# Top-k attention and a mixture of experts in one program: the routing of the first three batches is moved to earlier steps

## The chip, the cores and the metric

The kernel runs on one core of a Trainium2 chip. The metric is the device time of one execution in microseconds. Before the change it is 1211.64 us, the median of three runs (1211.17 to 1212.91). The engines are TensorE (PE), VectorE (DVE), ScalarE (ACT), GpSimd (POOL) and SyncE (SP, which issues most of the transfers); each works off its own queue in the order of the program and waits for others by semaphores.

## The reference

Two stages follow each other. The first is attention in which each query keeps its 32 highest scores; the second sends each of the 4608 rows to one of eight experts (the largest logit decides) and scales the expert's output by that expert's probability.

```python
# q, k, v: (8, 8, 576, 64); x: 4608 rows of 512
scores = scale * np.matmul(q, k.transpose(0, 1, 3, 2))
kth = np.partition(scores, -top_k, axis=-1)[..., -top_k:-top_k + 1]      # top_k = 32
scores = np.where(scores >= kth, scores, -1e9)
attn = np.exp(scores - scores.max(-1, keepdims=True)); attn /= attn.sum(-1, keepdims=True) + 1e-9
x = np.matmul(attn, v).transpose(0, 2, 1, 3).reshape(4608, 512)

logits = x @ w_gate + modality_bias[modality_id]
e_idx = np.argmax(logits, axis=1)
gate_w = softmax(logits)[np.arange(N), e_idx]
for e in range(8):                                                       # w1: 512 x 1024, w2: 1024 x 512
    out[e_idx == e] = gate_w[e_idx == e, None] * (np.maximum(x[e_idx == e] @ w1[e], 0) @ w2[e])
```

## The kernel before

Attention is cut into 288 tiles of 128 queries: a batch has four pairs of heads, a pair nine tiles, so a batch is 36 tiles. One loop over steps `i` is a software pipeline written out by hand. In step `i` PE makes the scores of tile `i + 2` and transposes the probabilities of tile `i - 9` (`TL` is 9); ACT copies the scores to SBUF, counts signs (tile `i - 3`, buffer `K`) and makes exponentials; POOL multiplies scores and signs (`pool_y`, tile `i - 4`); DVE searches the top 32 (`subs`, `chain`, `find`) and masks (`keep`, tile `i - 7`). For two of three tiles below 48 (`early`) DVE writes only a mask (`hide`), POOL adds it one step later (`hidden`, line 470) and ACT makes the masked exponentials (`masked`). Products with V (`av`) run once for four tiles of a pair (`role(u)` 3 and 7) and once for the ninth (8); those of role 7 go through a queue, `avs`, from which the next step takes them, the others run at once. Their results are copied to `xT` in the step after (`xev`).

The routing of a batch stands in the same loop, at a position `r` counted from `i - (TL + 2)` modulo 36. At `r` = 0 come the reciprocal sums and the product with the gate (`logits`), at 1 its transposes (`logit_rows`), at 2, 3, 3, 4, 4 the transposes of the five chunks of rows (`xrow`, `RXQ`). What DVE has to do with their PSUM tiles is put into `late` and runs one step after. At `r` = 2 the list of `route` goes into the queue `side`: seven DVE operations up to the one-hot rows `oh`, a `PAUSE` (the rest waits for the next step), the exponentials and `ranks` (ten small products of PE and a copy by ACT), a `PAUSE`, and nine operations up to `dest`. At `r` = 5 the scatters (`send`, an indirect transfer that POOL issues, one for each chunk) go into `posted`, or for batch 0 into `sends`; POOL issues two of them at the end of each step. Three pauses later `base` is raised and `done` sets `seen`, the number of rows that the experts may use; for batch 0 `done` follows the list of `route` at once.

The experts work in slots of 256 rows. `more_moe` starts a slot when `seen` allows it (`PB`: 2, 4 and 6 slots after one, two and three batches): `sched` chooses an expert and its rows on DVE, SP gathers the rows into `xg`, `tokens` reads them on DVE, and `expert` makes a list of PE units (transposes `xt`, 16 of `hid`, 16 of `outp`). A planner deals these units to the steps: `spare_pe` gains 3.4 (`STEP`) in a step less the estimated `cost` of the step's attention work and is held to at most 2.6 (`CAP`); units are taken while it is above zero. A unit of `hid` or `outp` counts 0.88, a step's attention work 1.00 to 4.95 (4.95 where products of role 7 and 8 meet, every ninth step). As long as nothing is seen, every step runs `keep_warm(NW)`, six products whose results nobody reads; one more such call stands ahead of the loop (line 998). After the loop the rest of the list is worked off, and the remaining six slots are done one by one with operands split into two parts (`slot`, lines 1057 and 1073).

The pool of PSUM tiles named X has three buffers in a ring; `prep` (transposes of k and q for the next pair, positions `PJ`), `av`, `logits`, `logit_rows`, `xrow` and `ranks` all take from it. DVE's work of a step is put in order by `arrange`, which knows an estimated use and delay of each kind.

Of the kernel before, what the change touches and what calls it, by code (L numbers as in the profile page):

```python
# [13 lines left out]
AF = mybir.ActivationFunctionType  # L14
# [15 lines left out]
NW = 3  # L30
# [14 lines left out]
TL = LR + 2  # L45
# [11 lines left out]
QO = 0  # L57
PJ0 = (1, 2, 3)
FAST = 7
RXQ = (2, 3, 3, 4, 4)  # L60
SNQ, RNQ = 12, 12
RLF = (0, 1)
# [13 lines left out]
def kernel(  # L76
# [13 lines left out]
    V, A, G, PE, SP = nc.vector, nc.scalar, nc.gpsimd, nc.tensor, nc.sync  # L90
    B, H, S, D = q.shape
    E, Dm, F = w1.shape
    N = B * S
    HP = H // 2
# [25 lines left out]
    PAUSE = lambda: None  # L120
# [96 lines left out]
    ohb = [const.tile([128, 5, E], BF, name=f"ohb{i}") for i in range(2)]  # L217
    for t in ohb:
        V.memset(t, 0.0)
    lgb = [const.tile([128, 5, E], FT, name=f"lgb{i}") for i in range(2)]  # L220
    for t in lgb:
        V.memset(t, 0.0)
    x5 = const.tile([128, 5, XW], FT, name="x5")
# [44 lines left out]
    bias_all = const.tile([128, B, 5, E], FT, name="bias_all")  # L268
# [85 lines left out]
    role = lambda i: (i - 1) % 9  # L354
# [31 lines left out]
    def sevac(i):  # L386
        T[i]["S"] = sb = wk.tile([128, S], FT, name="Ssb", bufs=LR + 1 + QL - QO)
        A.activation(sb.rearrange("p (a b) -> p a b", a=2), T[i]["ps"], AF.Copy, scale=0.125)  # L388
# [142 lines left out]
    def apart(s, before, reads=()):  # L531

        for o in [*before, *reads]:
            tc.declare_no_dep(s.ins, o, reason="other rows")
        before.append(s.ins)
        G.memset(spare, 0.0)
# [47 lines left out]
            late.append(lambda lt=lt, r=r, c0=c0, n=n: V.tensor_reduce(  # L584
                lg[:r, c0:c0 + n, :], lt[:r].rearrange("p c e a h -> p c e (a h)"), axis=AX.X, op=OP.add))

    def route(lg, bias, oh, x5b, wait=0):

        t5 = lambda nm: const.tile([128, 5], FT, name=nm)
        t40 = lambda nm: const.tile([128, 5, E], FT, name=nm)  # L590
        bc = lambda t: t[:, :, None].to_broadcast([128, 5, E])
        be = lambda t: t[:, None, :].to_broadcast([128, 5, E])
        l2, z, key, ez, pr, pb = t40("r_l2"), t40("r_z"), t40("r_key"), t40("r_ez"), t40("r_pr"), t40("r_pb")
        mx, km, sm, ps5 = t5("r_mx"), t5("r_km"), t5("r_sm"), t5("r_ps5")
        dest = const.tile([128, 5], I32, name="dest")
        st = {}

        def ranks():
            ps = psX.tile([128, 6, E], FT, name="X")
            st["ps"] = const.tile([128, 6, E], FT, name="r_rk")  # L600
            PE.matmul(ps[:, 0:5, :], tri, oh, start=True, stop=False, skip_group_check=True)
            for c in range(1, 5):
                PE.matmul(ps[:, c:5, :], onesb, oh[:, 0:5 - c, :], start=False, stop=False, skip_group_check=True)
            for c in range(5):
                PE.matmul(ps[:, 5, :], onesb, oh[:, c, :], start=(c == 0), stop=(c == 4), skip_group_check=True)
            A.activation(st["ps"], ps, AF.Copy)

        def send(c):
            n_ = 128 if c < 4 else 64
            apart(G.indirect_dma_start(  # L610
                out=xs[:ZROW, :], out_offset=bass.IndirectOffsetOnAxis(ap=dest[:n_, c:c + 1], axis=0),
                in_=x5b[:n_, c, :], in_offset=None), scat, reads)
            fresh.append(scat[-1])

        return [
            lambda: V.tensor_tensor(l2, lg, bias, op=OP.add),
            lambda: V.tensor_reduce(mx, l2, axis=AX.X, op=OP.max),
            lambda: V.tensor_tensor(z, l2, bc(mx), op=OP.subtract),
            lambda: V.scalar_tensor_tensor(key, z, 0.0, be(rev), op0=OP.is_equal, op1=OP.mult),
            lambda: V.tensor_reduce(km, key, axis=AX.X, op=OP.max),  # L620
            lambda: V.tensor_tensor(oh[:, 0:4, :], key[:, 0:4, :], bc(km)[:, 0:4, :], op=OP.is_equal),
            lambda: V.tensor_tensor(oh[:64, 4, :], key[:64, 4, :], km[:64, 4:5].to_broadcast([64, E]),
                                    op=OP.is_equal),
            PAUSE,
            *[PAUSE] * wait,
            lambda: A.activation(ez, z, AF.Exp),
            ranks,
            PAUSE,
            lambda: V.tensor_reduce(sm, ez, axis=AX.X, op=OP.add),
            lambda: V.tensor_scalar(sm, sm, EPS, None, op0=OP.add),  # L630
            lambda: V.reciprocal(x5b[:, :, GW], sm),
            lambda: V.tensor_tensor(pb, st["ps"][:, 0:5, :], be(base), op=OP.add),
            lambda: V.tensor_tensor(pr, pb, oh, op=OP.mult),
            lambda: V.tensor_reduce(ps5, pr, axis=AX.X, op=OP.add),
            lambda: V.tensor_scalar(dest, ps5, float(ZROW), None, op0=OP.add),
            lambda: G.tensor_scalar(x5b[:, :, TOK], tokb, 1.0, 1.0, op0=OP.mult, op1=OP.mult),
            lambda: G.tensor_scalar(tokb, tokb, float(S), 1.0, op0=OP.add, op1=OP.mult),
        ], [f for c in range(5) for f in [lambda c=c: send(c), PAUSE] + [PAUSE] * SP_[c]] + [
            lambda: V.tensor_tensor(base, base, st["ps"][:, 5, :], op=OP.add)]
# [316 lines left out]
    def keep_warm(n):  # L956

        ps = psE.tile([128, 512], FT, name="E")
        for _ in range(2 * n):
            PE.matmul(ps[:, :256].rearrange("p (a b) -> p a b", a=2), onesb, onesb[:, None, :].to_broadcast([128, 2, 128]), start=True, stop=True)  # L960
# [30 lines left out]
    for x in range(QL):  # L991
# [3 lines left out]
            qk(0, 0, qbd[0])  # L995
            keep_warm(KP)
        sevac(x)
    keep_warm(NW)
    ok = lambda x: 0 <= x < NT
    early = lambda u: u < EARLY and u % 3 != 2  # L1000
    dn_of = lambda u: den[(u // 36) % 2][:, (u // 9) % HP, role(u):role(u) + 1]
    PREP, PREP0 = dict(zip(PJ, "tkq")), dict(zip(PJ0, "tkq"))
# [107 lines left out]
    store = []  # L1110
    for i in range(LAST):
# [5 lines left out]
        p, j = divmod(i, 9)  # L1117
        u = i - TL
# [14 lines left out]
        u = i - (KL + 1)  # L1133
# [6 lines left out]
        u = i - LE  # L1140
# [6 lines left out]
        u = i - TL  # L1147
        if ok(u):
            evac(u)
        u = i - LR - 1  # L1150
# [8 lines left out]
                f()  # L1159
        cost += COST["rest"] * (len(lp) > 0)  # L1160
        part = (PREP if p else PREP0).get(j)
        if p + 1 < NPAIR and part:
            prep(p + 1, part)
            cost += COST["t" if part == "t" else "prep"]
        if p + 2 < NPAIR and j in LJ:
            load(p + 2, "kq"[LJ.index(j)])
        if j == VJ and p < NPAIR:
            load(p, "v")
        b1, r = divmod(i - (TL + 2), 36)
        b1 -= 1  # L1170
        if 0 <= b1 < B:
            if r == 0:
                chore.extend(recip(b1, den[b1 % 2]))
            early_route = lambda b: b < FAST or b == B - 1
            rl, rx = (RL, RX) if FAST <= b1 < B - 1 else (RLF, RXQ if b1 < FAST else RXF)
            if r == rl[0]:
                rows_of[b1] = logits(b1, xTs(b1))
                cost += COST["logits"]
            if r == rl[1]:
                logit_rows(b1, rows_of[b1], lgb[b1 % 2])  # L1180
                cost += COST["xrow"]
            for c in range(5):
                if rx[c] == r:
                    xrow(b1, c, xTs(b1), x5)
                    cost += COST["xrow"]
            if r == rl[1] + (1 if early_route(b1) else 2):
                steps, store = route(lgb[b1 % 2], bias_all[:, b1], ohb[b1 % 2], x5, int(FAST <= b1 < B - 1))
                side.extend(steps)

                def done(n=b1 + 1):  # L1190
                    seen[0] = n * S
                    fresh.clear()
                if b1 == 0:
                    side.extend([store.pop(), done])
            if r == max(rl[1], rx[4]) + (1 if early_route(b1) else 2):
                if b1 == 0:
                    sends.extend(f for f in store if f is not PAUSE)
                else:
                    side.extend([f if f is PAUSE else (lambda f=f: posted.append(f)) for f in
                                 ([x for x in store[:-1] if x is not PAUSE] if b1 < FAST else store[:-1])] +  # L1200
                                [PAUSE] * 3 * (b1 < FAST) + [store[-1], done])
        u = i - (TL + 1)
# [3 lines left out]
            cost += c  # L1206
        if ok(u) and role(u) in (3, 7, 8):
            f = av(u // 9, role(u), xTs(u // 36)[(u // 9) % HP])
            if role(u) == 7:
                avs.extend(f)  # L1210
            else:
                f[0][1]()
                avs.extend(f[1:])
                cost += f[0][0]
# [42 lines left out]
        small_ = []  # L1257
        quick = 0 <= b1 < FAST and r < 16
        for x in range((RNQ if quick else RN) if rush else 0):
# [15 lines left out]
        if ok(i - LR):  # L1275
            u = i - LR
# [105 lines left out]
    def slow():  # L1382
# [6 lines left out]
        with tc.For_i(0, B, 1) as b:  # L1389
# [30 lines left out]
            for part in route(lgb[0], sb[:, 0], ohb[0], x5):  # L1420
                for f in part:
                    f()
# [42 lines left out]
```

## Time and profile before

| | us |
|---|---|
| median of three runs | 1211.64 |
| the profiled execution | 1209.28 |
| its span, first to last instruction | 1207.6 |
| PE busy (products) | 1157.0 |
| DVE busy | 1104.1 |
| ACT busy | 983.4 |
| POOL busy | 677.7 |

The mean granted clock of PE over the span is 0.992. The ends of products are modelled, so a busy PE is not necessarily a PE at its peak. In the chain of work that ended last PE has 59% of the span and DVE 31%. Expert products of the loop are lines 796 and 808, those of the last six slots lines 1057 and 1073. A wait in the rows below is the idle time of an engine just before an instruction, in brackets behind it, with the one that ended it. Step numbers are not in the trace; one search of line 437 on DVE, one product of line 433 on POOL stand for one step.

### The profile page before, as it was taken

Reading aid. Unit: us, or ns where it says so; the run is one execution under the profiler, and the core shown is the slowest. Engines: PE = TensorE matmul, PEld = TensorE weight load, DVE = VectorE, ACT = ScalarE, POOL = GpSimd, SP = SyncE. Lnnn points to the kernel's source line nnn. Section 1 sums busy time; section 2 is a strip of 40 time slices with the busy share of each in tenths; the row PEclk is TensorE's granted clock in tenths of the full one; section 3 lists DMA queues with packets and bytes.
Section 4 is the critical chain, followed back from the end, with each engine's and each line's share of the span. In section 5 each row is a group of like instructions: output and inputs, shape, how many; then the busy total and the mean of one; then the engine's idle time right before and its main releaser. Section 6 shows DMA issues by size and latency. Waiting matters only on the chain.

```text
span 1207.6 us, 28111 instructions
## 1 busy us (share of the span) xinstructions
PE 1157.0 (96%) x7920; PEld 906.5 (75%) x7920; DVE 1104.1 (91%) x5562; ACT 983.4 (81%) x2015; POOL 677.7 (56%) x1256
## 2 busy tenths in 40 slices
PE   8889979999999998999999999999999999999998
PEld 6666767778677876878687777868787777589987
DVE  7999999999999999999999999999998999486772
ACT  5999978998888986998899899989998888355652
POOL 6888875564755565565656576556655666121011
PEclk9999999999999998999999999999999999999999
DMA  5653358663586637664675657665675653277750
GB/s 125 174 163 88 88 127 236 191 167 88 153 241 152 164 104 220 175 174 123 174 215 149 168 148 196 168 160 147 183 192 145 177 156 126 83 269 237 261 198 22
DMA packets 204324, 197.10 MB, mean 163 GB/s; under 512 B 104413, under 2 KB 151533, under 8 KB 204160
## 3 DMA queue, kind: packets, MB, share of 16 engines
q1 hardware_dynamic: 196880, 175.92, 54.0%
q0 software_dynamic: 6080, 19.00, 4.3%
q8 instruction: 66, 1.08, 0.4%
q14 instruction: 98, 0.80, 0.2%
q10 hardware_dynamic: 1200, 0.30, 0.1%
HBM read 118.63 MB, written 24.23 MB: 118 GB/s over the span
## 4 chain that ended last, share of the span: by engine, by line
PE 59%; DVE 31%; ACT 5%; issue 2%; DMA 1%; POOL 0%; SPq 0%; POOLq 0%; ACTq 0%; DVEq 0%
PE E L796 11%; PE E L808 11%; PE X L519 8%; DVE cand L395 8%; PE S L383 7%; PE T L491 6%; DVE mg L437 5%; DVE P L457 5%; PE X L1073 5%; PE X L1057 4%; DVE cand L406 2%; DVE cand L407 2%; PE E L1057 1%; DVE mg L408 1%; PE X L317 1%
## 5 line engine op out<-in xcount | busy, mean ns | idle before, releaser
L395 DVE MAX8 cand<-Ssb 128x8 f32<-128x96 f32 x1728 | 388.1, 244 | 1.8 <-ACT Ssb L388 1.8
L433 POOL TENSOR_TENSOR y<-Ssb,K 128x576 f32<-128x576 f32 x288 | 368.7, 1280 | 30.5 <-ACT K L427 30.1
L383 PE MATMUL S<-ks,qs 128*128 128x288 f32 x992 | 221.1, 345 | 18.7 <-ACT Ssb L388 12.9
L427 ACT ACTIVATE K<-Ssb,n 128x576 bf16<-128x576 f32 x288 | 229.9, 798 | 7.3 <-POOL y L433 6.9
L388 ACT ACTIVATE Ssb<-S 128x576 f32<-128x576 f32 x284 | 187.8, 661 | 53.5 <-PE S L383 23.8
L437 DVE MAX8 mg<-y 128x8 f32<-128x576 f32 x288 | 213.3, 741 | 4.2 <-POOL y L433 4.2
L796 PE MATMUL E<-xgT,w1b 128*128 128x256 f32 x832 | 201.1, 384 | 2.6 <-ACT hT L800 1.5
L451 ACT ACTIVATE ex<-Ssb,sm 128x576 f32<-128x576 f32 x256 | 202.3, 790 | 0.0
L383 PEld LDWEIGHTS S<-ks,qs 128*128 128x128 f32 x992 | 152.1, 190 | 66.8 <-issue 26.2
L457 DVE SCALAR_TENSOR_TENSOR P<-Ssb,kth,ex 128x576 f32<-128x576 f32 x230 | 193.7, 842 | 6.8 <-ACT ex L451 5.6
L499 ACT ACTIVATE PT<-T 128x640 f32<-128x640 f32 (+1 forms) x288 | 193.5, 672 | 5.8 <-PE T L491 5.8
L808 PE MATMUL E<-w2b,hT 128*128 128x512 f32 x416 | 194.2, 595 | 0.5 <-ACT hT L800 0.2
L491 PE MATMUL T<-idf,P 128*128 128x128 f32 x1152 | 169.5, 274 | 7.2 <-ACT P L476 6.6
L796 PEld LDWEIGHTS E<-xgT,w1b 128*128 128x128 f32 x832 | 151.0, 190 | 29.5 <-ACT hT L800 7.4
L480 POOL TENSOR_SCALAR spare<-P 1x1 f32<-1x1 f32 x230 | 41.7, 181 | 196.6 <-DVE mg L406 166.7
L519 PE MATMUL X<-PT,vm 128*64 128x256 f32 (+1 forms) x1536 | 147.3, 334 | 1.2 <-DVE x L553 1.2
L491 PEld LDWEIGHTS T<-idf,P 128*128 128x128 f32 x1152 | 137.2, 140 | 13.8 <-ACT P L476 10.7
L519 PEld LDWEIGHTS X<-PT,vm 128*64 128x64 f32 x1536 | 89.1, 138 | 46.4 <-issue 12.5
L420 POOL TENSOR_SCALAR n<-mg 128x1 f32<-128x1 f32 x288 | 71.2, 247 | 92.5 <-DVE mg L408 70.1
L808 PEld LDWEIGHTS E<-w2b,hT 128*128 128x128 f32 x416 | 73.3, 190 | 61.9 <-issue 58.1
L1079 POOL DMA_INDIRECT out_dram<-ot,tk x12 | 12.3, 1022 | 101.9 <-ACT ot L1078 101.9
L427 ACT ACTIVATION_READ_ACCUMULATOR K<-Ssb,n 128x1 f32 x288 | 63.7, 221 | 0.0
(234 smaller groups left out, 2166.1 us busy)
## 6 DMA issues: line engine op xcount, KB each, us to landing
w1b<-in_moe_w_dram SPq DMA_DIRECT2D x76, 512.0 KB, 5.7
w2b<-in_moe_w_dram SPq DMA_DIRECT2D x76, 512.0 KB, 5.1
ks<-st SPq DMA_DIRECT2D x62, 288.0 KB, 4.3
ks<-st SPq DMA_DIRECT2D x62, 256.0 KB, 4.5
qs<-st SPq DMA_DIRECT2D x124, 128.0 KB, 5.3
xg<-xs SPq DMA_DIRECT2D x19, 516.0 KB, 4.1
vm<-in_v_dram SPq DMA_DIRECT2D x32, 256.0 KB, 5.1
km<-in_k_dram SPq DMA_DIRECT2D x63, 128.0 KB, 3.6
```

What stands on the lines that cost most here:

```text
L383: PE.matmul(ps[:, hf, :288], l, m, start=(n == 0), stop=(n == len(terms) - 1))
L395: return [lambda s=s: V.max(c[:, s * 8:s * 8 + 8], T[i]["S"][:, bnd[s]:bnd[s + 1]]) for s in range(NSUB)]
L427: A.activation(t["K"], t["S"], AF.Sign, scale=2.0 ** -24 - 1.0, bias=t["n"][:, 1, i % 3:i % 3 + 1], accum_out=t["n"][:, 0, i % 3:i % 3 + 1])
L433: G.tensor_tensor(t["y"], t["S"], t["K"], op=OP.mult)
L437: V.max(t["mg"][:, i % 3, 24:32], t["y"])
L451: A.activation(t["ex"], t["S"], AF.Exp, bias=t["s"][:, i % 3:i % 3 + 1])
L457: V.scalar_tensor_tensor(t["P"], t["S"], kth[:, i:i + 1], t["ex"], op0=OP.is_ge, op1=OP.mult, accum_out=dn)
L491: PE.transpose(T[i]["pt"][:, x, :], (Pm if c == 4 else Pb[c % 2])[:, h * 512 + x * 128:h * 512 + x * 128 + 128], idf)
L499: A.activation(o, T[i]["pt"][:, :n], AF.Copy)
L519: PE.matmul(o.rearrange("p (a b) -> p a b", a=2) if j < 8 else o, l, r, start=(c == 0), stop=(c == 4))
L796: PE.matmul(ps[:, f % 2], w1b[:, c, f * 128:(f + 1) * 128], xgT[:, c, :], start=(c == 0), stop=(c == KC - 1))
L808: PE.matmul(o["py"], hT[:, f, t * 128:(t + 1) * 128], w2b[:, f, :], start=(f == 0), stop=(f == FC - 1))
```

## The change

It concerns batches 0, 1 and 2 (`SOON = 3`), and one call ahead of the loop.

- The position `r` of a batch's routing is counted from `TL + 1`, one step sooner; batches 3 to 7 keep `TL + 2`.
- The last products with V of such a batch (role 7, `u % 36 == 35`) run at once, not through `avs`.
- In `route` the first `PAUSE` goes, and `ranks` stands ahead of the exponentials: the ranks are issued in the step of the one-hot rows.
- The scatters are put into their queue at `r` = `rx[2] + 1` = 4, where the third chunk is done, not at 5.
- In the step in which the logits now stand the transposes of k for the next pair are left out; they run one step later.
- `keep_warm(NW)` ahead of the loop goes.

```diff
+SOON = 3
-    def route(lg, bias, oh, x5b, wait=0):
+    def route(lg, bias, oh, x5b, wait=0, soon=False):
...
-            PAUSE,
-            *[PAUSE] * wait,
-            lambda: A.activation(ez, z, AF.Exp),
-            ranks,
+            *[PAUSE] * (wait + 1 - soon),
+            *[lambda: A.activation(ez, z, AF.Exp), ranks][::-1 if soon else 1],
             PAUSE,
...
         sevac(x)
-    keep_warm(NW)
...
         part = (PREP if p else PREP0).get(j)
+        if 1 <= p // HP <= SOON and p % HP == 1 and j in (1, 2):
+            part = PREP.get(1) if j == 2 else None
...
-        b1, r = divmod(i - (TL + 2), 36)
+        b1, r = divmod(i - (TL + 1), 36)
+        if b1 > SOON:
+            b1, r = divmod(i - (TL + 2), 36)
         b1 -= 1
+        soon = b1 < SOON
...
-                steps, store = route(lgb[b1 % 2], bias_all[:, b1], ohb[b1 % 2], x5, int(FAST <= b1 < B - 1))
+                steps, store = route(lgb[b1 % 2], bias_all[:, b1], ohb[b1 % 2], x5, int(FAST <= b1 < B - 1), soon)
...
-            if r == max(rl[1], rx[4]) + (1 if early_route(b1) else 2):
+            if r == (rx[2] + 1 if soon else max(rl[1], rx[4]) + (1 if early_route(b1) else 2)):
...
             f = av(u // 9, role(u), xTs(u // 36)[(u // 9) % HP])
-            if role(u) == 7:
+            if role(u) == 7 and not (u % 36 == 35 and u // 36 < SOON):
                 avs.extend(f)
             else:
                 f[0][1]()
```

## Rows read from the trace of the kernel before

**Rows 1.** The page's first part: busy us, share of the span, instructions.

```profile
PE 1157.0 (96%) x7920; PEld 906.5 (75%) x7920; DVE 1104.1 (91%) x5562; ACT 983.4 (81%) x2015; POOL 677.7 (56%) x1256
```

**Rows 2.** By stage: length, each engine's busy us and instructions, granted clock, DMA share.

```profile
144.00:199.00 55.00, 45.59 (x371) 36.84 (x373) 52.05 (x292) 43.20 (x98) 37.35 (x61) 0.94 0.55 148
199.00:1015.00 816.00, 800.87 (x5359) 614.79 (x5358) 796.18 (x4232) 718.01 (x1486) 487.92 (x944) 1.00 0.62 167
1015.00:1190.00 175.00, 172.67 (x1119) 146.60 (x1116) 117.02 (x302) 93.20 (x151) 33.48 (x66) 1.00 0.56 189
```

**Rows 3.** Timeline of the start: start us, us, engine, line, operation, tiles.

```profile
10.64 1.70 PE L960 MATMUL E<-onesb 128*128 128x256 bf16 x12
...
11.17 0.64 ACT L388 ACTIVATE Ssb<-T 128x576 f32<-128x576 f32 x1
...
21.51 0.76 DVE L437 MAX8 mg<-y 128x8 f32<-128x576 f32 x1 [0.76 <-POOL y L433]
```

**Rows 4.** The loop with experts, by line: 796 and 808 (PE), 437 (DVE).

```profile
199.00:1015.00 816.00, 184.64 (x764) 138.83 (x764) 1.00 0.62 167
...
199.00:1015.00 816.00, 179.25 (x384) 67.81 (x384) 1.00 0.62 167
...
199.00:1015.00 816.00, 169.69 (x229) 1.00 0.62 167
```

**Rows 5.** Around the loop's end: the chain that ended last, then PE's timeline.

```profile
1054.15 6.18 PE E L808 x14
...
1068.44 0.39 PE L1057 MATMUL X<-xgh,w1h 128*128 128x256 f32 x1 [0.36 <-DVE hl L1060]
```

**Rows 6.** Timeline of POOL and DVE after batch 0.

```profile
177.42 0.98 POOL L610 DMA_INDIRECT xs<-x,dest  x1
...
178.84 1.27 POOL L470 TENSOR_TENSOR ex<-Ssb,hT 128x576 f32<-128x576 f32 x1
...
180.27 1.28 POOL L610 DMA_INDIRECT xs<-x,dest  x1 [0.15 <-issue]
...
181.60 1.28 POOL L433 TENSOR_TENSOR y<-Ssb,K 128x576 f32<-128x576 f32 x1
...
182.91 0.76 DVE L437 MAX8 mg<-y 128x8 f32<-128x576 f32 x1 [2.05 <-POOL y L433]
```

**Rows 7.** The first slot's rows: the chain that ended last, then PE's timeline.

```profile
180.27 4.88 DMA xs<-x,dest
185.16 3.38 DMA xg<-xs
...
188.69 0.63 PE L774 MATMUL E<-idf,xg 128*128 128x128 f32 x4 [0.81 <-DMA xg<-xs]
```

**Rows 8.** DVE's waits (us, times, longest) of 270 to 300 and 400 to 480 us.

```profile
DVE lt L581 <- PE X L573: 2.1, 1, 2.1
...
DVE lt L581 <- PE X L573: 1.6, 1, 1.6
```

**Rows 9.** Ranks: timelines of DVE and PE in batch 0; ACT's waits in all.

```profile
160.67 1.95 PE L519 MATMUL X<-PT,vm 128*64 128x256 f32 x16 [1.16 <-DVE x L553]
...
163.11 0.66 DVE L553 TENSOR_TENSOR x<-X,rd 128x512 f32<-128x512 f32 x1
...
163.82 0.18 PE L601 MATMUL X<-ohb,tri 128*128 128x40 bf16 x1
...
ACT r_rk L606 <- PE X L605: 20.4, 8, 3.6
```

**Rows 10.** After batch 2: PE's timeline, the stretch behind it, DVE's waits.

```profile
456.38 1.11 PE L786 MATMUL X<-idf,xg 128*128 128x128 f32 x4 [4.91 <-DMA xg<-xs]
...
455.00:463.00 8.00, 6.62 (x32) 4.51 (x32) 7.97 (x47) 3.15 (x6) 5.76 (x9) 0.57 1.02 290
...
DVE Pm L457 <- ACT ex L451: 0.6, 1, 0.6
DVE P L457 <- ACT ex L451: 0.6, 1, 0.6
```

## The prediction

> **What bounds the kernel now.** I read the busy line of the page first [rows 1]: PE 96% and DVE 91% are both near full, so the share alone does not name the limit. The table by stage does [rows 2]. From 199 to 1015 us DVE is busy 796 of 816 us: the attention loop goes at DVE's pace, 816 us for 229 steps (one top-k search on line 437 each), 3.56 us a step, and PE is filled up to that pace with expert work. From 1015 to 1190 us it is the other way round: DVE is busy for 117 of 175 us, PE for 172.7. So work that PE has done before the loop's end comes off the tail at full price, while inside the loop only time in which DVE stands idle can be gained. From 144 to 199 us, where the first batch is routed and the experts start, DVE is idle for 3 of 55 us and the granted clock is below one.
>
> **Part 1, one warming call less.** Before the loop six of twelve adjoining warm-up products go. All twelve run from 10.64 to 12.34 us, so six are about 0.8 us of PE; what follows them needs the second score tile copied out, which ends at 11.17 + 0.64 = 11.81 us [rows 3]. PE can go on at 11.81 instead of some 12.3: 0.4 us. DVE still waits once after that, 0.76 us for POOL's product at 21.51 [rows 3], which hangs on that chain, so the 0.4 us can arrive. I take -0.4; bounds 0 and -0.8.
>
> **Part 2, expert work two steps sooner.** With `TL + 1` for `TL + 2` every routing step of batches 0 to 2 comes one step sooner, and with the one-hot rows and the ranks in one step another step goes: for batch 0 `seen` is set at i = 49, not 51, for batches 1 and 2 `done` runs at r = 7 of an origin one step sooner, not r = 8. Scatters go two steps sooner as well, so from slot 0 to slot 5 the whole train moves up by two steps. What are two steps worth? Expert products of lines 796 and 808 take 184.6 + 179.3 us of PE in 229 steps [rows 4], 1.59 us a step, 3.2 us for two. Does the gain reach the end? The slots that wait for a batch (0, 2, 4) wait for the three batches that move, slot 6 starts well after batch 3 is seen, so the lead is kept, if no later gate swallows it. At the end it shortens the expert products that are left after the loop: a run of 14, 6.18 us, 0.44 each [rows 5]; 3.2 us are seven of them. Behind them another chain is close: the first product of the split slot's second half waits 0.36 us for DVE at 1068.44 [rows 5], and DVE has splits and a choice of slot to do first, so a little may stick there. I take -3.0; bounds 0 (lead swallowed) and -4.7 (the two added steps are cheap in the planner's accounts, costs 1.00 and 1.11 of 3.4 us).
>
> **Part 3, scatters behind three chunks.** In batch 0 two of three tiles are masked on POOL (`early`, line 470), and the same POOL queue issues the scatters. A pair of scatters, the second at 177.42, a masked tile at 178.84, the fifth scatter at 180.27, and only then the product that DVE's search needs, at 181.60: DVE waits 2.05 us [rows 6]. POOL's load in such a step is 1.27 + 1.28 + 2.2 + small ones, some 5.1 us, against DVE steps of 3 to 4 us there. Moved up, the pairs of scatters end steps 50 and 51, in which DVE itself has two row products of 0.66 us [rows 9] and ten to twelve choosing steps besides its 3.1 us, more than 5 us; the fifth scatter falls into step 52, whose tile (44) isn't masked on POOL. So POOL should keep up, and the 2.05 us go. Next late is the gathered block: the last scatter to its landing 4.88 us, then the gather 3.38 us [rows 7]. PE's transposes waited for it only 0.81 us at 188.69 [rows 7], because 4.95 us (by the planner's costs) of value products stood ahead of them in that step; at i = 53 only some 1.4 us do, so PE will now idle 5 us or more. DVE reads the same block in step 54, about when it lands (some 8.3 us after the scatter, against 6.5 us to the step's start and 1.8 us into it). I take -2.0 in all; bounds -2.9 (two smaller idle stretches behind it go too) and +1.2 (below).
>
> **Part 4, logits and value products.** Taking the last value products of a batch out of the queue only moves 2.45 us (planner's cost) from step 46 to step 45; the logits still follow them by one step. In batches 1 and 2 DVE waits for the logit rows 2.1 and 1.6 us [rows 8]. From the start of step 81 to those rows PE now has, by the planner's costs, 1.11 + 4.95 + 2.42 + 2.0 and 2.64 of expert work, 13.1 us in three steps and a part; then 3.56 + 3.27 + 2.0 and 0 to 1.8 of expert work, 8.8 to 10.6, for a DVE that comes one step (3.1 us) sooner. That gives waits of 1.2 to 3.0 us: none gained, 0; bounds -0.9 and +1.4 a batch. The transposes of k are put one step later, behind the logits; their copies to `ks` land in 4.3 us and have five steps: 0. SP's queue keeps its order.
>
> **Part 5, ranks in the step of the one-hot rows.** Today the ranks' PSUM buffer is freed by the row product at 163.11 of the next DVE step; PE gets to them at 163.82, and ACT, with everything queued behind the copy, waits for them 20.4 us in the eight batches, 2.55 us each [rows 9]. In the new order the buffer before is freed by the small logit product, ahead of the one-hot rows, so PE waits for those alone. Queued behind PE's wait: the next step's scores; behind ACT's: the sign, the exponentials, the score copy. DVE has two steps of scores in hand. I take 0; bounds -1 and +3.7 a batch (ACT's mean wait of 2.55 passed on to DVE, and a wait for a row buffer as the one of 1.16 us at 160.67 [rows 9]).
>
> **Sum.** -0.4 - 3.0 - 2.0 = -5.4 us on the profiled execution's 1209.28 us, 1203.9. The median of the runs is 2.36 us above that execution, so I forecast 1211.64 - 5.4 = **1206.2 us**.
>
> **The rivals.** (a) *PE's new idle stretch before the gather costs clock.* In batch 2 PE already stood 4.91 us before such a block, and from 455 to 463 us the granted clock was 0.57, between its two levels of 1.2 and 2.4 GHz [rows 10]; PE fell behind, and DVE waited twice 0.6 us for exponentials in the steps after [rows 10]. The same at i = 53 gives 1207.4 us. The Trainium skill speaks against the change here: TensorE: Matmul & The Clock Gate, section "Why this matters for your kernels", advises to leave no long idle gaps between bursts of products, since the clock falls back; rows 10 agree. 0.15. (b) *POOL still late*: the masked tiles of steps 50, 51 and 53 meet the scatters in place of those of 53 and 54, and the 2.05 us stay: 1208.2 us. 0.13. (c) *The lead is swallowed*, by a gate in the loop or by DVE's chain in the tail: only -2.4 is left, 1209.2 us. 0.16. (d) *Slower*: PE in order at the ranks. All row buffers turn in a ring of three, and in the new order the k and q copies, the first row product and the ranks follow each other in it one step tighter; if PE's waits, 2.55 + 1.16 us, reach DVE in each of three batches, 11.1 us are lost and 5.4 won: 1217.3 us. It decides from 1.8 us a batch. Against it: PE has 55 - 45.6 = 9 us to spare in the first [rows 2], and the waits stand on ACT today without a wait of DVE behind them. 0.10. That the change does not start the experts sooner is excluded by the order written out in the loop.
>
> **The numbers.** My forecast has 0.46 with its near variants (a logit wait more or less, batch 2's gather wait avoided, down to 1202). The range holds the forecast and (a) to (c) with their spread: 1201.5 to 1211.0. A measurement of this kernel tells 0.2%, 2.4 us, from no change: faster is below 1209.2. The forecast, (a), (b) and half of (c) are faster, 0.82, of which I take 0.03 away for the unknown logit waits; the other half of (c), those 0.03 and a fifth of (d) are no change; most of (d) is slower. 0.79, 0.13, 0.08.
>
> **What would show it.** Right: the expert products' first block about 6 to 7 us sooner against the steps; no wait of DVE for POOL's product in batch 0; the ranks' copy on ACT waiting under 1 us in three batches; a run of some seven expert products after the loop instead of 14. Wrong: waits of DVE on the gathered block or the row buffers of over 1.8 us in each of the first three batches; the same 14 products after the loop; granted clock under 0.8 over the stretch in which the first slot starts.

## The result, and the profile after

The changed kernel takes 1225.67 us (median of 5 runs, 1223.16 to 1226.75) against 1211.64 us (5 runs, 1210.99 to 1213.59): 1.0104 of the time before, interval 1.0086 to 1.0122. It is slower, by 13 to 14 us, where 5.4 us faster was forecast. The profiled execution of after took 1223.16 us with a span of 1221.5; that of before is 13.9 us shorter in span.

Lines of the changed kernel are one higher than those of before up to the attention functions (406 is now 407) and one or two lower behind them (808 is 807, 1057 is 1055). The page of after: span, busy time by engine (answers to [rows 1]), and the engines' shares of the chain that ended last.

```profile
span 1221.5 us, 28083 instructions
PE 1156.5 (95%) x7902; PEld 907.1 (74%) x7902; DVE 1109.9 (91%) x5562; ACT 982.9 (80%) x2015; POOL 678.5 (56%) x1256
PE 48%; DVE 31%; DMA 9%; ACT 7%; issue 3%; SPq 2%; POOL 0%; POOLq 0%; ACTq 0%; DVEq 0%
```

PE is busy for as long as before, DVE 5.8 us longer. What is new is DMA at 9% and SP's queue at 2% of the chain; before they had 1% and 0%. A transfer became the limit somewhere. Where it did is found by laying the two traces step against step. A step n is here the stretch from the first search of one tile's candidates on DVE (the first `mg<-cand`, line 406, 407 after) to that of the next; there are 288. From these rows, worked out for the two profiled executions (us; "stretched" is explained in the last section):

| steps | before | after | difference | DVE idle, before and after | stretched DVE operations |
|---|---|---|---|---|---|
| 1 to 47 | 140.8 | 139.8 | -1.0 | 2.0, 1.7 | 1, 0 |
| 48 to 61, first batch routed | 57.8 | 58.4 | +0.6 | 2.9, 2.9 | 2, 1 |
| 62 to 71 | 31.8 | 39.7 | **+7.9** | 0.0, 5.8 | 0, 3 |
| 72 to 83 | 39.2 | 40.9 | +1.7 | 0.0, 1.3 | 1, 1 |
| 84 to 167 | 312.5 | 313.1 | +0.6 | 9.5, 10.6 | 8, 10 |
| 168 to 287 | 422.8 | 425.7 | +2.9 | 10.3, 9.4 | 7, 14 |
| 288 to the end | 192.6 | 193.1 | +0.5 | | |

With 0.7 us by which the first step starts later this is the 13.9 us. More than half of it lies in ten steps, and there in one: step 64 takes 8.5 us in place of 3.4. PE's and ACT's timelines of after around it (start us, us, engine, line, operation; in brackets the idle time before and what ended it), and below them the table by stage (length, busy us of PE, PEld, DVE, ACT, POOL, granted clock, DMA share, GB/s):

```profile
218.10 1.30 PE L384 MATMUL S<-ks,qs 128*128 128x288 f32 x4 [3.91 <-DMA kqt<-in_k_dram]
...
219.43 0.65 ACT L389 ACTIVATE Ssb<-S 128x576 f32<-128x576 f32 x1 [5.33 <-PE S L384]
...
186.00:190.00 4.00, 4.00 (x22) 3.52 (x21) 3.76 (x25) 2.77 (x8) 1.07 (x2) 0.83 0.01 4
190.00:194.00 4.00, 4.00 (x50) 3.04 (x49) 4.00 (x25) 3.07 (x9) 2.20 (x5) 1.00 0.02 4
194.00:198.00 4.00, 3.93 (x27) 3.50 (x26) 3.68 (x16) 4.00 (x9) 1.31 (x2) 1.00 0.21 60
206.00:210.00 4.00, 4.00 (x25) 3.64 (x24) 4.00 (x22) 3.00 (x8) 1.87 (x4) 1.00 1.08 226
```

PE waits 3.9 us for the first score product of a pair that reads the stacks `ks` and `qs`; ACT cannot copy the scores out, DVE runs out of scores, and PE's idle time costs clock as well (0.57 from 218 to 222 us). The profile names a load of k that landed last; the product itself reads `ks` and `qs`. The DMA engines carry nothing for 8 us and little for 12, from 186 to 198 us, and are full from 198 to 218 us (DMA share 0.95 to 1.08 in the stages of 4 us). SP's timeline shows why: before (first fence) and after (second).

```profile
192.26 5.48 SPq L333 DMA_DIRECT2D ks<-st  x6
199.16 0.39 SPq L728 DMA_DIRECT2D w1b<-in_moe_w_dram  x1
199.75 0.37 SPq L732 DMA_DIRECT2D w2b<-in_moe_w_dram  x1
200.23 2.45 SPq L335 DMA_DIRECT2D qs<-st  x4
```

```profile
179.63 0.37 SPq L731 DMA_DIRECT2D w2b<-in_moe_w_dram  x1
195.89 0.38 SPq L727 DMA_DIRECT2D w1b<-in_moe_w_dram  x1
196.78 0.38 SPq L731 DMA_DIRECT2D w2b<-in_moe_w_dram  x1
197.26 6.08 SPq L334 DMA_DIRECT2D ks<-st  x6
203.55 0.57 SPq L731 DMA_DIRECT2D w2b<-in_moe_w_dram  x1
204.43 0.38 SPq L727 DMA_DIRECT2D w1b<-in_moe_w_dram  x1
205.66 0.35 SPq L706 DMA_DIRECT2D xg<-xs  x1
206.49 0.37 SPq L731 DMA_DIRECT2D w2b<-in_moe_w_dram  x1
208.12 3.06 SPq L336 DMA_DIRECT2D qs<-st  x4
```

From 188 us on six expert transfers of some 512 KB each stand ahead of `qs` where there were two (five weight loads and a gather of rows, `xg`), the first two of them ahead of `ks`. The four more are 2.1 MB, at the 226 GB/s of that stretch 9 us; `qs` goes out 7.9 us later. There was little to spare: in before the first two of the four moves of `qs` landed at 207.1 and 207.5 us (the landings of the other two are not in the trace), and the product that reads them ran at 209.63. And SP, which works in order, issued nothing at all from 180 to 196 us: it stood at the choice of the next slot and at a weight buffer that PE had not yet read out. Its waits from 178 to 200 us (us in all, times, longest):

```profile
SPq L702 <- DVE er L698: 8.0, 1, 8.0
SPq L727 <- PE E L795: 7.3, 1, 7.3
```

### The profile page after: what moved, and what is told of

The parts are those of the page before. It is cut to its first block, busy times and chain, and to the rows that moved or that the text cites. A ratio compares the mean times of both kernels' runs of the same rounds, so it can differ in the third digit from the quotient of the medians.

```text
span 1221.5 us, 28083 instructions
## 1 busy us (share of the span) xinstructions
PE 1156.5 (95%) x7902; PEld 907.1 (74%) x7902; DVE 1109.9 (91%) x5562; ACT 982.9 (80%) x2015; POOL 678.5 (56%) x1256
## 3 DMA queue, kind: packets, MB, share of 16 engines
q8 instruction: 66, 1.08, 0.4%
## 4 chain that ended last, share of the span: by engine, by line
PE 48%; DVE 31%; DMA 9%; ACT 7%; issue 3%; SPq 2%; POOL 0%; POOLq 0%; ACTq 0%; DVEq 0%
DVE cand L396 8%; PE E L795 8%; PE E L807 7%; PE X L520 7%; PE S L384 6%; DVE mg L438 5%; DVE P L458 5%; PE T L492 5%; PE X L1071 4%; PE X L1055 4%; ACT Ssb L389 2%; DVE cand L407 2%; DVE cand L408 2%; DMA qs<-st 2%; ACT K L428 2%
## 5 line engine op out<-in xcount | busy, mean ns | idle before, releaser
L421 POOL TENSOR_SCALAR n<-mg 128x1 f32<-128x1 f32 x288 | 74.0, 257 | 87.9 <-DVE mg L409 65.0
```

## The experiments

Theory (queue): since the experts start two steps sooner while the pairs of heads keep their steps, the expert loads of the first slots are issued ahead of the moves of pair 7's stacks, in SP's one queue; the stacks come late and the scores wait. Rivals: TensorE's clock after its wait for the gathered block; the later transposition of k; the warming that is gone; sheer traffic, whatever its order; the earlier logit rows and ranks. All runs are compared with runs of the kernel before on the same chip (medians 1211.98 to 1212.99 us), the ratio is the one to go by; a profile or a table by step is of one execution, which can lie some us off its kernel's median (in experiment 9, 7.2 us above it: it is the slowest of its twelve).

**1. The new order switched off** (only the warming call is gone).

```diff
-SOON = 3
+SOON = 0
```

> The changed kernel with its new order switched off for all three batches (SOON = 0), so that against the kernel before only the warming products of the start are gone. Queue theory (the loss comes from the expert work of the first batch, which now starts two steps sooner and puts weight loads that must wait for a buffer ahead of the moves of the k and q stacks in SP's queue): nothing of that is left, 1211.2 us, between 1210.8 and 1211.7, and no wait of the scores S for qs at step 64. Rival (part of the 14 us comes from the warming that is gone: a lower clock or a later start, the first step began 0.7 us later): above 1213 us.

1211.61 us, ratio 1.0001 (0.9991 to 1.0011). Step 64 is as before. The warming products neither cost nor give anything that can be measured. By the two profiles steps 168 to 287 take 424.0 us, against 422.8 in before with the same order: two executions can differ by 1.2 us there.

**2. The stacks' moves first in each step.**

```diff
+        for f in moves:
+            f()
         arrange(ops, *end)
-
-        for f in moves:
-            f()
```

> The changed kernel, but in each step the moves of the k and q stacks are issued ahead of the step's small operations, so that they stand ahead of that step's expert loads and choices in SP's queue. Queue theory: the moves of step 56 to 58 go out at about 192 and 200 us instead of 197 and 208, PE's wait of 3.9 us at 214 us and the 5.0 us that VectorE idles in step 64 are gone: 1217 to 1219 us. Traffic theory (the 16 DMA engines are full from 199 to 218 us whatever the order, so the stacks land late anyway): the wait stays over 3 us and the time at 1224 to 1227. Theory of the later k (the transposition of k one step later is what delays the stacks): unchanged, 1224 to 1227.

1248.52 us, ratio 1.0299 (1.0283 to 1.0316): none of the three. In the stage in question the wait for `qs` went, but at 220.41 us PE waited 3.08 us for the next pair's raw k and q, whose loads now stood behind the same weights; and from step 140 on this order loses in every batch (DVE idle 40 us in steps 140 to 287 against 13); why is not shown. The order in the queue matters, but putting one transfer first only hands the wait to the next.

**3. The first batch declared routed two steps later.**

```diff
-                    side.extend([store.pop(), done])
+                    side.extend([store.pop(), PAUSE, PAUSE, done])
```

> The changed kernel with all its parts, but the first batch is declared routed two steps later, so that the gather, the expert loads and the expert products of the first slots start in the steps in which they do in the kernel before. Queue theory: the 8.0 us of steps 62 to 68 and the 1.6 us of steps 73 to 76 go, 1214 to 1217 us. If the loss comes from the unqueued products with V, the earlier ranks or the later k, whose places are not changed here: 1224 to 1227 us.

1214.73 us, ratio 1.0015 (1.0000 to 1.0030). Steps 62 to 71 take 31.8 us, DVE is not idle there. The loss of the first batch comes from the experts' early start, not from its logits, ranks or k, which keep their new places here.

**4. k transposed in its old step.**

```diff
-        if 1 <= p // HP <= SOON and p % HP == 1 and j in (1, 2):
+        if False:
```

> The changed kernel with the transposition of k back in its old step (no step later in pairs 5, 9 and 13). Queue theory: pair 7's stacks are not touched by it, the wait at step 64 stays (3 to 5 us of VectorE idle), 1224 to 1227 us. Theory of the later k: the loss or most of it goes, 1213 to 1218 us.

1228.88 us, ratio 1.0136 (1.0120 to 1.0152): 3 us slower still, and the stall of step 64 stays. The later k pays, given the earlier logits: without it steps 48 to 61, 84 to 97 and 120 to 133 are 0.6, 1.4 and 1.5 us longer, and DVE's waits for the logit rows of the three batches, none, 1.8 and 2.6 us in after, are 1.2, 3.3 and 3.9.

**5. PE's wait for the gathered block filled with warming products.**

```diff
             if cc == 0:
+                if s == 0 and c == 0:
+                    keep_warm(30)
```

> The changed kernel with 60 warming products put on TensorE just ahead of the first expert's transposes, in the place where it waits 8.6 us for the gathered block. At the 0.14 us that one takes they fill 8.3 us of that wait. Clock theory (the wait drops the granted clock to 0.50 until 186 us, so that the first expert's products of step 55 take 3.7 us where the same twelve took 2.8, the second half of k's stack and its moves come later, and the queue of loads behind them too): the clock stays at 1.00, steps 54 and 55 shorten by 2 to 4 us, the moves of k go out by 193 us and the stall of step 64 is smaller by as much or gone: 1217 to 1222 us. Queue and traffic theory (SP is held and the loads pile up because of the early start itself): the stall of step 64 stays over 3.5 us, 1223 to 1226 us.

1225.46 us, ratio 1.0110 (1.0088 to 1.0131). PE's timeline, and its waits from 178 to 222 us:

```profile
173.02 6.71 PE L961 MATMUL E<-onesb 128*128 128x256 bf16 x60
181.70 0.63 PE L775 MATMUL E<-idf,xg 128*128 128x128 f32 x4 [1.97 <-DMA xg<-xs]
...
183.79 2.76 PE L797 MATMUL E<-xgT,w1b 128*128 128x256 f32 x12
...
PE S L384 <- DMA kqt<-in_k_dram: 4.0, 1, 4.0
```

The clock stays at 1.00 (174 to 190 us) and the twelve products take 2.76 us instead of 3.74, as the clock theory wants. The stall and the time stay all the same: 1 us is won by step 59 and nothing at the end. The clock did fall, but it is not the cause of the loss.

**6. The first expert's products two steps later, everything else early.**

```diff
-                rush.extend(pick + [begin] + l1[:2] + done + [PAUSE, sent] + rows + go + [PAUSE, l1[2], l1[3], PAUSE] + tok)
+                rush.extend(pick + [begin] + l1[:2] + done + [PAUSE, sent] + rows + [PAUSE, l1[2], l1[3], PAUSE] + go + tok)
```

> The changed kernel, but TensorE gets the first expert's transposes and products two steps later, while the choice, the scatters, the gather and the first weight loads stay at their new, early places; warming products go on in between. If it is the products in TensorE's order that do the harm (TensorE stands 8.6 us at the gather, its clock falls, and the products stand ahead of the k transposition): the stall of step 64 goes, 1213 to 1217 us, as with the first batch declared routed two steps later (1214.7). If it is the early loads: 1222 to 1227 us.

1213.73 us, ratio 1.0007 (0.9995 to 1.0019). The first weights and rows still come early (169.9 and 178.3 us) and harm nobody. The loads fall into other places too: three of `w2b` go out from 180.0 us, in the time in which SP issued nothing in after, and only two weight loads stand between the moves of `ks` and of `qs`, which goes out at 197.1 us. So this run alone does not tell products from loads; the next two hold loads alone.

**7 and 8. All products early, only the weight loads behind the stacks.** The loads of `w1b` and `w2b` that fall into steps 56 to 58 are put in a list and issued at the end of step 58, behind the moves of `qs`; in the second kernel those of steps 56 to 60 at the end of step 60, behind the loads of the next k and q too. (These are values of `i` in the loop; in the traces the held loads go out one or two steps later by the count of the table.)

```diff
+    def now(f):
+        held.append(f) if 56 <= i <= 58 else f()
+
     def load_w1(s, g):
         SL[s]["w1"][g] = len(moe)
-        SP.dma_start(w1b[:, :, g * 256:g * 256 + 256],
+        now(lambda: SP.dma_start(w1b[:, :, g * 256:g * 256 + 256],
...
         for f in moves:
             f()
+        while i == 58 and held:
+            held.pop(0)()
```

> The changed kernel, its expert products, scatters and gathers all at their new, early places; only the five expert weight loads of 512 KB that SP would issue in steps 56 to 58 are held and issued right behind the moves of the k and q stacks of step 58. If the stall of step 64 is made by the weights that stand ahead of the stacks of pair 7 in SP's queue: the score products no longer wait for qs. The loads of the next k and q then stand behind 2.5 MB, so a stall of up to 4 us may come at step 66 in its place, as with the moves put first (3.9 us): 1219 to 1226 us. If it is the early products in TensorE's order that delay the stacks: the stall of step 64 stays over 3 us, 1224 to 1227 us.

> The same with the weight loads held until the end of step 60, so that they stand behind the stacks of pair 7 and behind the loads of the next k and q. Queue theory: neither step 64 nor step 66 waits for a transfer, the 8 us of steps 62 to 72 go, 1215 to 1219 us; the second products of the first expert may wait for their weights, at most 3 us. If the early products in TensorE's order are the cause: 1222 to 1227 us.

1222.68 us, ratio 1.0095 (1.0069 to 1.0121), which its interval does not tell from after, and 1219.34 us, ratio 1.0054 (1.0032 to 1.0075), 0.3 us above what the queue theory allowed. With the hold to step 58 the scores don't wait, but PE waits for the raw q instead:

```profile
218.58 0.30 PE L311 MATMUL X<-idf,kqt 128*128 128x128 f32 x1 [2.28 <-DMA kqt<-in_q_dram]
```

With the hold to step 60 DVE is idle for 0.4 us in steps 62 to 71 against 5.8, and the time falls by 6.3 us. SP's timeline of it:

```profile
196.49 5.53 SPq L334 DMA_DIRECT2D ks<-st  x6
203.18 0.36 SPq L706 DMA_DIRECT2D xg<-xs  x1
203.63 2.43 SPq L336 DMA_DIRECT2D qs<-st  x4
206.16 1.30 SPq L143 DMA_DIRECT2D km<-in_k_dram  x2
```

The same bytes and the same products, in another order of issue: that shows the queue, for 6 of the 14 us. It is not all. The moves of `ks` are hardly earlier than in after (196.5 against 197.3 us): k's second half comes out of PE behind twelve early expert products. And steps 62 to 83 still take 75.0 us against 69.9 with the products held; 1.7 us of that is idle DVE and 2.7 us four stretched operations, of which the kernel of experiment 6 has none there. SP does not stand at a weight buffer in this run and `ks` still goes out at 196.5 us, so what that stand costs by itself is not shown. Why the early products bring these is not settled.

**9. The first batch in the old order, batches 1 and 2 in the new.**

```diff
-        if 1 <= p // HP <= SOON and p % HP == 1 and j in (1, 2):
+        if 2 <= p // HP <= SOON and p % HP == 1 and j in (1, 2):
...
-        if b1 > SOON:
+        if b1 not in (2, 3):
...
-        soon = b1 < SOON
+        soon = 1 <= b1 < SOON
...
-            if role(u) == 7 and not (u % 36 == 35 and u // 36 < SOON):
+            if role(u) == 7 and not (u % 36 == 35 and 1 <= u // 36 < SOON):
```

> The changed kernel with the first batch in its old order and only batches 1 and 2 in the new one. If the loss belongs to the first batch's start: no stall at step 64, and what is left is what batches 1 and 2 bring by themselves, 1210 to 1215 us. If every batch loses a part: above 1216 us.

1217.20 us, ratio 1.0041 (1.0025 to 1.0058): above 1216, as was expected if every batch loses a part. Batches 1 and 2 lose by themselves. PE's longest wait from 343 to 360 us is of the kind known by now:

```profile
PE S L384 <- DMA kqt<-in_k_dram: 3.4, 1, 3.4
```

Four loads of `w2b` of slot 2, issued from 327.45 us, stand ahead of `qs` (331.59); before, `qs` went out at 326.32. This stall is not a part of after's 14 us: steps 100 to 112 take 42.1 us in before and 42.9 in after, but 49.9 here, 50.4 in experiment 6 and 48.8 in experiment 3. Of the runs here it came up only where the first batch's stall is gone.

**10. The same, with second-weight loads held.** Those of steps 94 to 96 and 130 to 132 are issued at the end of steps 96 and 132, behind the stacks and the next k and q:

```diff
+        held.append(f) if i in (94, 95, 96, 130, 131, 132) else f()
...
+        while i in (96, 132) and held:
+            held.pop(0)()
```

> Batches 1 and 2 in the new order, the first in the old one (that kernel took 1217.2 us, 4.7 above the kernel before: score products waited 3.4 us for a stack at 345 us, behind four second-weight loads of 512 KB that SP issued ahead of the q stack's moves in step 94). Here the second-weight loads of steps 94 to 96 and 130 to 132 are held until the k and q loads of those steps have been issued. If batches 1 and 2 lose by the same queue as the first: 1211 to 1214 us, and no wait of over 1 us for qs in steps 98 to 104. If they lose by the earlier ranks and logit rows (waits of VectorE at the batch's boundary): 1215.5 to 1218 us.

1209.12 us, ratio 0.9977 (0.9961 to 0.9993), below what either theory allowed. By eight loads in another place 8 us are won, and batches 1 and 2 turn from a loss into a gain; steps 100 to 112 take 42.5 us. In before the same loads stand behind the stacks and the next k and q without a hold (`w2b` from 337.68 us, behind the last load of q at 336.80). ACT's wait for scores from 318 to 362 us, which was 6.5 us with 4.5 at once, is now

```profile
ACT Ssb L389 <- PE S L384: 1.4, 2, 1.0
```

The earlier logit rows and ranks, unchanged between the two, are not what cost.

**11 to 13. Versions that beat both.** The first batch alone in the new order (`SOON = 1`), with the hold of experiment 3 and with that of experiment 6; then all three batches, with the hold of 6 and the second-weight loads held as in 10.

> Only the first batch in the new order, and declared routed two steps later, so that its experts start in their old steps; batches 1 and 2 in the old order. The kernel with all three batches and this hold was 2.2 us ahead of the kernel before by step 77 and lost that and more in steps 100 to 121 and later. If that loss belongs to the new order of batches 1 and 2: 1208.5 to 1211 us, the lead of 2 us kept. If it comes later whatever batches 1 and 2 do (VectorE's small operations meeting GpSimd's y more often): 1211 to 1214 us.

> Only the first batch in the new order, batches 1 and 2 in the old one, and TensorE gets the first expert's products two steps after the gather was issued (choice, scatters, gather and first weight loads stay early). By the runs so far the stage from step 48 to 84 is then 1.5 us shorter than before, and batches 1 and 2 add nothing: 1209 to 1211 us, like the kernel with the first batch declared routed two steps later (1209.5). If the early transfers get in the way of other loads: 1212 to 1215 us.

> All three batches in the new order, the first expert's products two steps after its gather (1213.7 us in that form), and the second-weight loads of steps 94 to 96 and 130 to 132 held behind the q stack's moves and the next k and q loads. If the rest of the loss is the queue of batches 1 and 2: 1206 to 1210 us, faster than the first batch alone in the new order (1208.7). If it is the boundary work of batches 1 and 2: 1212 to 1215 us.

1209.51 us, ratio 0.9974 (0.9960 to 0.9988); 1208.74 us, ratio 0.9966 (0.9951 to 0.9981); and 1206.54 us, ratio **0.9949** (0.9930 to 0.9967). The last has the lowest median of this study, 6 us under the one before and 19 under the change as it was made; its interval overlaps that of the version before it. Its steps 100 to 112 still take 45.6 us.

## Why the prediction was wrong

The forecast was 1206.2 us, the range ended at 1211.0, and none of the rivals held the time; the slower one gave 1217.3, and for another reason.

**The step that failed** is in part 4: "their copies to `ks` land in 4.3 us and have five steps: 0. SP's queue keeps its order." That priced the moves of `ks` against their own step only, and those of `qs` not at all. The queue does not keep its order, and it is part 2 that breaks it: a train that moves up by two steps takes its loads along past everything that keeps its step. The loads were left out of part 2's sum altogether; it counted products (seven of 0.44 us) and no bytes. Had they been counted, they were four transfers of 512 KB past the moves of `qs`, 9 us at the rate of that stage, against some 2 us that `qs` had to spare there in before. Measured: the moves go out 7.9 us later, and steps 62 to 71 are 7.9 us longer (that the two are the same number is chance; step 64 alone is 5.1 us longer). The 1.7 us of steps 72 to 83 come from the early start as well (38.3 and 38.1 us there in experiments 3 and 6); the rest, some 4 us from step 84 on, has no cause shown.

**Part 1, -0.4:** within the measurement (experiment 1).

**Part 2, -3.0:** the lead was there and came to nothing. In after the loop does more expert work (this group of the table by line, 199 to 1028 us, has 774 products where [rows 4] has 764 to 1015 us), and the run behind the loop is 10 products instead of the 14 of [rows 5]: the chain that ended last, PE's timeline, and the line of the table.

```profile
1068.76 4.31 PE E L807 x10
...
1072.89 1.04 PE L1026 MATMUL X<-idf,xg 128*128 128x128 f32 x8
1075.31 0.36 PE L1055 MATMUL X<-xgh,w1h 128*128 128x256 f32 x1 [1.38 <-POOL spare L537]
1076.71 0.39 PE L1055 MATMUL X<-xgl,w1h 128*128 128x256 f32 x1 [1.05 <-DVE xgl L1011]
...
L795 PE MATMUL E<-xgT,w1b 128*128 128x256 f32 x774 | 188.0, 385 | 2.5 <-ACT hT L799 1.3 <-ACT ot L817 0.5
```

But the first split product starts 46.9 us into step 288, against 46.5 before (1061.51 us): PE waits 1.4 and 1.1 us for the split rows, and from the start of step 288 to the end it is 193.1 against 192.6 us. Rival (c), the lead swallowed by the chain of splits in the tail, came true there, though not its time. In the kernel of the lowest median the first expert's products start in their old steps, the run behind the loop is 14 again, and the tail 192.5 us: its gain is not this term.

**Part 3, -2.0:** the mechanism was right. DVE's waits for GpSimd's product fell, and the gathered block took their place, as the working said it would. DVE's waits in the whole of after (before: 4.2 us for `y` in four waits, and [rows 6]), and PE's timeline, which answers to [rows 7]:

```profile
DVE sgt L718 <- DMA xg<-xs: 2.1, 1, 2.1
DVE mg L438 <- POOL y L434: 0.7, 1, 0.7
...
181.39 1.09 PE L773 MATMUL E<-idf,xg 128*128 128x128 f32 x4 [8.61 <-DMA xg<-xs]
```

PE's wait was 8.6 us, as "5 us or more" allowed. The size was -2.0 + 2.1, about nothing in after; with the first expert held back (experiments 6, 11 and 12) steps 48 to 83 are 1.5 to 2.6 us shorter than before.

**Part 4, logits, 0, and part 5, ranks, 0:** near. DVE waits 1.8 and 2.6 us for the logit rows of batches 1 and 2 where [rows 8] have 2.1 and 1.6: -0.3 and +1.0, inside the bounds of -0.9 and +1.4. ACT's waits for the ranks fell from the 20.4 us of [rows 9] to 15.7 (in the first three batches from 7.9 to 1.2). That k is moved was put at nothing; without it the change is 3 us slower (experiment 4).

**Rival (a), the clock,** came true in its first half: 0.50 from 174 to 186 us, the lower of the two levels. The Trainium skill's advice against idle gaps (TensorE: Matmul & The Clock Gate, "Why this matters for your kernels") describes what the rows show, but filling the gap won nothing (experiment 5). **Rival (d)**, PE in order at the ranks, did not show: experiment 10 has those ranks in batches 1 and 2, the last version in all three, and both are faster than before.

So the change's idea was sound in part. The kernel with the first expert held back and the second weights put back behind the stacks takes 1206.5 us. That this is close to the forecast is luck: the -3.0 us of part 2 are not in it. One term of the sum was missing, the loads, and two came to nothing in after (parts 2 and 3).

## What to carry to other kernels

When a stage is moved, list for each in-order queue what its instructions pass and what passes them, transfers above all: here moves that waited for nothing themselves were late by the 2.1 MB that were issued ahead of them. Price the cover of a transfer in the queue it will stand in, not in the steps it has. If an early start is wanted, let the issue of what is needed next go first and hold back only the bulk loads; holding eight of them won 8 us here (experiment 10), more than the 5.4 us that the change was to win.

## What the runs showed of the hardware

**Small operations of VectorE can last until GpSimd's product beside them ends.** In the stages without a stall after still loses time, and DVE is busy 5.8 us longer with the same operations. `eq<-i9s,n` and `jk<-eq,mg` (lines 445 and 446 of after, 96 of each) alone take 8.1 us more in sum, others less. DVE's timeline of after, then POOL's:

```profile
746.52 0.16 DVE L445 TENSOR_TENSOR eq<-i9s,n 128x27 f32<-128x27 f32 x1
...
755.99 0.96 DVE L445 TENSOR_TENSOR eq<-i9s,n 128x27 f32<-128x27 f32 x1
...
755.63 1.28 POOL L434 TENSOR_TENSOR y<-Ssb,K 128x576 f32<-128x576 f32 x1 [0.95 <-ACT K L428]
```

The one of 0.96 us began inside POOL's `y` and ended with it (756.9 us); the other lies outside any. Of the 36 `eq` of after that began inside a `y`, the 8 that began in its first 0.05 us took 0.17 us, 25 ended 41 to 49 ns after it did, and three began in its last 0.07 us. Of `jk`, the 8 that began inside a `y` took 0.99 to 1.15 us, the 88 others 0.17 in the median. Searches (MAX8, 0.24 us) take the same inside and outside. Such stretched operations (of a kind whose median is under 0.4 us, over 0.3 us longer than that median, more than half inside a `y`) are 19 in before (15.2 us beyond the medians) and 29 in after (20.4 us) up to step 287; the versions of experiments 12 and 13 have 18 and 21. Most read two tiles, but `rd<-den` and the copy `sgt<-xg`, which read one, are among them (0.82 us of `rd` inside, 0.17 outside). Their number differs with the order: from step 168 on, where the order is the old one again, after has 14 of them (9.8 us) and before 7 (5.6 us), a difference of 4.2 us where 2.9 us are lost. That this is what they cost was not tried by itself. The Trainium skill (GPSIMD Engine Reference, "1. Specifications") says that GpSimd's way to SBUF is shared with VectorE and that instructions with two SBUF inputs contend; the rows of `eq` and `jk` agree, and give the size.

**A small move on SP's queue came late by the bulk loads issued ahead of it.** With 16 engines full from 198 to 218 us the 128 KB moves of `qs`, issued from 208 us behind six bulk transfers, were waited for until 218; issued from 197 (experiment 6) or 200 us (before) behind two, no product waited for them. In before such a move landed 6.8 us after its issue in a queue nearly as full.
